# Spreading the tail frequencies late: VectorE for six token tiles, Pool for ten, and a new order of every engine's work

## The chip, the cores and the metric

The kernel runs on one core of a Trainium2 chip. Its five engines run their own instruction streams in order and meet only at semaphores: TensorE (PE in the profile, PEld its weight loads), VectorE (DVE), ScalarE (ACT), GpSimd (POOL) and SyncE (SP), which here only issues transfers. The metric is the device time in microseconds.

## What is computed

The reference, cut to what matters:

```python
def _A_ref(x, w_r, w_i):                       # spectral filter
    X = rfft2(x.astype(float32))               # over 2048 tokens and 576 features
    return irfft2(X * (w_r + 1j * w_i), s=(2048, 576)).astype(bfloat16)

def _B_ref(x, w_gate, w_up, w_down):           # 576 -> 4608 -> 576
    return (gelu(x @ w_gate) * (x @ w_up)) @ w_down

h  = x + _A_ref(layernorm(x), w_r, w_i)
h2 = h + _B_ref(layernorm(h), w_gate, w_up, w_down)
```

## The kernel before

The 2048 tokens form 16 tiles of 128 (token 16p + c lies on partition p of tile c). All Fourier transforms are matmuls with tables.

**Stage one** (to about 21 us) loads x, takes the layer norm's statistics, scales the token transform's table by 1/sigma for each tile (ATS) and multiplies (M, line 574). The tiles come in six groups (2, 2, 3, 3, 3, 3). For each group there are five products k, evicted from PSUM to U. A negated copy XN and a copy XR of x serve as operands.

**Stage two** (to about 46 us) works by 16 frequency groups: the feature transform (D its first part, d its second, line 649, evicted as CUS), a small transform (B, line 662, evicted as YS, named b), the product with the filter (T, line 674, giving TP; written "x" it reads PSUM directly and b is left out), and the transform back among the tokens of a group (V, line 682, evicted to V). The features of a filter row are 288; 256 go through V, and the last 32, the tails, go another way: Z copies them from TP to ZR, four groups together, R (line 697) multiplies them, and the result has to be spread into VR, where the inverse feature transform finds it in the layout [tile, k, group, e]. Of the 128 partitions, 32 belong to each of the four groups of a set; the spread (line 701) multiplies the product by a mask MK (1 on a group's 32 partitions, else 0), so that the other groups' places hold zeros. It is one DVE instruction for each half, over all 16 tiles: 512 elements for four groups.

**Stage three** (to about 57 us) does the inverse transform for the first six tiles (NPRE = 6): I (line 780), its copy GS, N (line 823), the addition to x (line 840), the squares for the second layer norm (s on ACT, S on DVE), q and c (square root and reciprocal), n and e (normalisation into HN, by DVE and POOL), the turn by PE (D and z, line 885, copied to HT), and the first gate and up matmuls (g and h, line 921).

**The feed-forward** (from about 57 us) is 4 blocks of 512 tokens by 36 slices of the hidden width: gate and up (line 921), gelu on ACT (929), product on DVE (930), then down (1022). The other ten tiles' inverse transform is deferred: it is put between the down matmuls of block 0 (`def_i`, line 939, reads V and VR; the first at 126 us).

**What sets the order.** Three strings of words are the order of all engines' instructions: SEQ1 for stage one, SEQF for stage two, SEQ for stage three. A word is a letter for the step, a number for its tile or group, and for some steps a letter for the engine (A ACT, D DVE, P POOL). Instructions are issued in that order on each engine, and waits follow from the data (class Prog). In SEQ1, S and Q are sums and sums of squares of a tile on ACT, B and b the statistics of a tile's halves on DVE, v q c variance, root and reciprocal of a group, m a helper of v, x the scaling, n and t the copies XN and XR, k idle matmuls that keep PE going, E an eviction to U (number 5i + j for group i and its j-th product), and F the later half of an eviction that was split. PSUM has 8 banks: `a_bank` hands them out in stage one, and in stage two `take` gives each D, B, V and R a pair of banks, by the oldest use.

The program order in every queue follows the strings, and transfers too: POOL's queue issues half of the second weight slot behind its last Z copy, then w_down's nine loads.

Of the kernel before, what the change touches and what calls it, by code (L numbers as in the profile page):

```python
# [23 lines left out]
SEQ1 = """b0 B1 Q3 t1 n0 t0 b1 k14 S3 B0 B2 v0 q0 b2 m3D c0 v1 B5 S4 b5 q1 k104 x0A M0 Q4 n1 n2 b6 c1 E2A B6 m4P B7 v2 k202 x1P q2 E1A E3A b7 B9 c2 E0A b9 M1 t2 E4A E5A b8 x2P B8 E6A b10 S13 M2 n3 E7A n4 v3 E8A B11 B10 B12 q3 Q13 c3 b11 x3A b12 t3 v4 b14 E9A B15 q4 E10A E11A m13P c4 E13A M3 t4 B14 x4P E12D E15A b15 t5 v5 E14A q5 E17A n5 E16D c5 x5A E18D E19A M4 E20D E21D M5 E24D E23A E26D F23A E22A F24A E28A E29A E25D F25A F29A E27D F26D F28D F22A F27A""".split()  # L24
# [3 lines left out]
SEQF = """D0 D1 d0 D2 d1 D3 d2 d3D B0 D4 b0D b1 D5 T1 d4 T0 d5 B1 b2 b3D T3 D6 V0 d6 B2 T2 Z0 b5 D7 D8 b4D Z1D Z2P d7 d8 Z3P T4 R0 V1 V2D B3 b6 T5 Z4D V3 b7 D10 D9 d10 Z5D T6 R1 d9 D11 V6 d11 Z6P B4 T7 b8 b9D V5 V4 B5 D12 T8 T9 D14 Z7D b10 b11 d12 T10 D13 Z8P d14 T11 d13 R2 D15 Z9P d15 B6 b12D Z10P b13 V7 T12 V9 V8 T13 B7 b14 b15x V10 Z11 Z12P T15x T14 Z13P Z14P Z15P V11 V12 V13 R3 V14 V15 R4""".split()  # L28
SEQ = """I0 I1 N0 I2 N1 s0 I3 S1 q0 N2 c0 s2 n0 N3 q1 n1 I5 e0 e1 c1 I4 z0 s3 n2 D1 e2 N5 q2 c2 N4 n3 D2 g10 e3 g00 h10 z3 h00 g20 g11 h20 g01 h11 g21 h01 h21""".split()
# [311 lines left out]
def _build(nc, A_x, A_w_r, A_w_i, B_w_gate, B_w_up, B_w_down, out):  # L341
# [194 lines left out]
    def ln1_scale(i, eng):  # L536
        c0, c1 = GROUPS[i]
        if eng == POOL:
            P.op(POOL, lambda g, c0=c0, c1=c1: g.tensor_tensor(ATS[:, c0:c1, :], ATB[:, :].unsqueeze(1).to_broadcast([128, c1 - c0, 128]),  # L539
                                                               RS1[:, c0:c1].unsqueeze(2).to_broadcast([128, c1 - c0, 128]), op=ALU.mult),  # L540
                 r=[("RS1", i), "ATB"], w=[("ATS", c) for c in range(c0, c1)])
        elif eng == ACT:
            for c in range(c0, c1):
                P.op(ACT, lambda a, c=c: a.activation(ATS[:, c, :], ATB[:, :], ACTF.Copy, scale=RS1[:, c:c + 1]),  # L544
                     r=[("RS1", i), "ATB"], w=[("ATS", c)])
        else:
            for c in range(c0, c1):
                P.op(DVE, lambda v, c=c: v.tensor_scalar(ATS[:, c, :], ATB[:, :], RS1[:, c:c + 1], None, op0=ALU.mult),
                     r=[("RS1", i), "ATB"], w=[("ATS", c)])
# [38 lines left out]
    def x_neg(i):  # L588
        c0, c1 = GROUPS[i]
        P.op(POOL, lambda g: g.tensor_scalar(XN[:, c0:c1, :], XO[:, c0:c1, 288:544], -1.0, 1.0, op0=ALU.mult, op1=ALU.mult),  # L590
             r=[("X", c) for c in range(c0, c1)], w=[("XN", c) for c in range(c0, c1)])

    def x_tail(i):
        c0, c1 = GROUPS[i]
        x = XO[:, c0:c1, 544:576]
        src = bass.AP(x.tensor, x.offset, [list(x.ap[0]), list(x.ap[1]), [0, 2], [-288, 2], [1, 32]])
        P.op(POOL, lambda g: g.tensor_copy(XR[:, c0:c1, :, :, :], src), r=[("X", c) for c in range(c0, c1)], w=[("XT", c) for c in range(c0, c1)])
# [93 lines left out]
    def st_R(q, b):  # L691
        j0, j1 = (4 * q - 3, min(4 * q + 1, NG)) if q else (0, 1)
        n, sp_, zb = j1 - j0, int(q == 0), (q - 1) % 2 if q else 2
        for k in range(4):
            for h in range(2):
                h0, vt = 64 * h, (0, 1, 1, 2)[k]
                P.op(PE, lambda t, k=k, h=h, h0=h0, vt=vt: t.matmul(bank(b + h, 0, 128, 0, 128), ZR[h0:h0 + 64, zb, k, :, :].rearrange("p a k -> p (a k)"),
                                                                    VT[h0:h0 + 64, sp_, vt, :].rearrange("p (k n e) -> p n k e", k=2, n=16), start=(k == 0), stop=(k == 3)),
                     r=[("ZR", zb, j) for j in range(4)] + ["VT"], w=[("PS", b + h)])
        for h in range(2):  # L700
            P.op(DVE, lambda v, h=h: v.tensor_tensor(VR[:, :, :, j0:j1, 4 * h:4 * h + 4].rearrange("p n k g e -> p (n k) g e"),
                                                     bank(b + h, 0, 128, 0, 128).rearrange("p (a e) -> p a e", e=4).unsqueeze(2).to_broadcast([128, 32, n, 4]),
                                                     MK[:, 0:n].unsqueeze(1).unsqueeze(3).to_broadcast([128, 32, n, 4]), op=ALU.mult),
                 r=[("PS", b + h), "MK"], w=[("V", g, 2) for g in range(j0, j1)])

# [6 lines left out]
    for w in SEQF:  # L712
# [15 lines left out]
        elif w[0] == "R":  # L728
            st_R(i, FB["R", i])
# [29 lines left out]
    vkeys = vk[0] + vk[1] + vk[2]   # L759
# [333 lines left out]
```

## Time and profile before

| | us |
|---|---|
| median of 3 runs | 488.54 |
| lowest and highest | 488.03, 488.96 |
| the profiled execution, its time | 489.37 |
| its span, first to last instruction | 487.6 |

The granted TensorE clock was 1.000. The profile names an instruction by line and engine, with the tile that it writes and those that it reads; times are counted from the start of the span. "Idle before" is the time in which the engine stood still ahead of an instruction, with what released it. Matmuls overlap, so their durations add up to more than the time that passes. The busy time of a group counts overlapping parts once; the mean of one does not.

### The profile page before, as it was taken

What the parts mean: (1) busy time and instruction counts of PE and PEld (TensorE: products, weight loads), DVE (VectorE), ACT (ScalarE), POOL (GpSimd) and SP (SyncE); (2) the same over time, 40 slices, a digit from 0 to 9 for tenths busy, and PEclk for the clock granted to TensorE, in tenths of its full rate; (3) what the DMA queues carried; (4) which work ended last, traced back from release to release, by engine and by line L of the source; (5) the groups of instructions that cost most, each with busy time, mean ns of one, the idle gap of its engine ahead of it and who ended that gap; (6) DMA issues with size and microseconds to landing.
All of it is one profiled execution on the core that took longest, in us unless ns stands there. A gap on an engine that the chain in (4) does not pass through costs nothing.

```text
span 487.6 us, 10636 instructions
## 1 busy us (share of the span) xinstructions
PE 480.4 (99%) x4726; PEld 282.1 (58%) x4726; DVE 191.9 (39%) x376; ACT 148.4 (30%) x296; POOL 33.8 (7%) x65
## 2 busy tenths in 40 slices
PE   7999999999999999999999999999999999999998
PEld 3767744444688744444577644444677444444775
DVE  6798733433576534333311144333211233333011
ACT  6988743223222222232200022332100123323000
POOL 5505420000000010000000000000000000000000
DMA  8978999100001071100000001000000000000000
GB/s 271 212 194 246 327 349 336 27 12 2 1 22 39 18 231 23 23 1 1 0 20 20 14 21 23 13 1 1 7 20 18 7 1 1 1 1 2 13 18 20
DMA packets 26174, 31.20 MB, mean 64 GB/s; under 512 B 11760, under 2 KB 17904, under 8 KB 26128
## 3 DMA queue, kind: packets, MB, share of 16 engines
q1 hardware_dynamic: 23872, 21.23, 15.5%
q0 software_dynamic: 2256, 9.29, 5.6%
q8 instruction: 37, 0.61, 0.5%
q14 instruction: 9, 0.07, 0.1%
HBM read 26.18 MB, written 2.36 MB: 59 GB/s over the span
## 4 chain that ended last, share of the span: by engine, by line
PE 93%; ACT 3%; DVE 1%; DMA 1%; SPq 0%; issue 0%; DVEq 0%
PE PS L921 57%; PE PS L1022 29%; PE PS L649 2%; DMA XO<-in_A_x_dram 1%; PE PS L939 1%; PE PS L574 1%; PE PS L662 1%; PE PS L682 1%; ACT V L639 1%; ACT U L585 1%; PE PS L957 1%; PE PS L780 0%; DVE XO L840 0%; SPq L251 0%; ACT OS L814 0%
## 5 line engine op out<-in xcount | busy, mean ns | idle before, releaser
L921 PE MATMUL PS<-HT,WG 64*128 64x512 bf16 (+1 forms) x2160 | 228.7, 371 | 0.0
L921 PEld LDWEIGHTS PS<-HT,WG 64*128 64x128 bf16 x2160 | 105.1, 94 | 121.8 <-issue 0.7
L930 DVE TENSOR_TENSOR AT<-GL,PS 128x512 bf16<-128x512 bf16 (+1 forms) x147 | 99.5, 677 | 177.5 <-ACT GL L929 177.4
L929 ACT ACTIVATE GL<-PS 128x512 bf16<-128x512 f32 (+1 forms) x147 | 86.5, 589 | 262.5 <-PE PS L921 251.3
L1022 PE MATMUL PS<-WD,AT 128*128 128x288 bf16 (+2 forms) x1152 | 144.9, 286 | 0.0
L1022 PEld LDWEIGHTS PS<-WD,AT 128*128 128x128 bf16 x1152 | 110.7, 98 | 30.6 <-ACT GL L929 1.3
L921 PE MATMUL PS<-HT,WGX 64*128 64x512 bf16 x486 | 53.4, 376 | 0.0
L1025 DVE TENSOR_TENSOR OS<-PS,XO 128x288 bf16<-128x288 f32 (+2 forms) x32 | 14.6, 457 | 94.4 <-PE PS L1022 94.3
L921 PEld LDWEIGHTS PS<-HT,WGX 64*128 64x128 bf16 x486 | 23.8, 94 | 28.7
L944 ACT ACTIVATE EB<-PS 128x288 f32<-128x288 f32 x10 | 4.1, 411 | 27.7 <-PE PS L939 27.7
L649 PE MATMUL PS<-FT,U 64*128 64x288 bf16 x160 | 12.1, 284 | 0.1
L513 DVE BATCH_NORM_STATS2 ST<-XO 128x6 f32<-128x288 bf16 x26 | 10.2, 442 | 3.4 <-DMA XO<-in_A_x_dram 3.4
L574 PE MATMUL PS<-ATS,XO 128*128 128x128 bf16 x96 | 9.2, 220 | 2.2 <-POOL ATS L539 1.2
L674 DVE TENSOR_TENSOR TP<-YS,WS 128x1152 bf16<-128x1152 bf16 x15 | 11.0, 762 | 0.1
L962 DVE TENSOR_TENSOR XO<-PS,XO 128x576 bf16<-128x576 f32 x10 | 7.6, 756 | 8.0 <-PE PS L957 8.0
L950 DVE TENSOR_TENSOR QB<-PS,EB 128x288 f32<-128x288 f32 x20 | 8.2, 452 | 3.4 <-ACT EB L944 3.3
L574 PEld LDWEIGHTS PS<-ATS,XO 128*128 128x128 bf16 x96 | 6.7, 97 | 4.8 <-ACT ATS L544 2.4
L639 ACT ACTIVATE CUS<-PS 128x576 bf16<-128x576 f32 x15 | 9.2, 652 | 0.8 <-PE PS L649 0.6
L867 DVE TENSOR_SCALAR HN<-XO,NM,RS 128x576 bf16<-128x576 bf16 (+1 forms) x28 | 9.3, 369 | 0.0
L649 PEld LDWEIGHTS PS<-FT,U 64*128 64x128 bf16 x160 | 6.6, 94 | 3.8 <-ACT CUS L639 0.7
L585 ACT ACTIVATE U<-PS 128x256 bf16<-128x256 f32 (+2 forms) x27 | 8.8, 423 | 0.1
L682 PE MATMUL PS<-VT,TP 64*128 64x128 bf16 x256 | 8.6, 217 | 0.1
(87 smaller groups left out, 205.5 us busy)
## 6 DMA issues: line engine op xcount, KB each, us to landing
WD<-in_B_w_down_dram POOLq DMA_DIRECT2D x9, 576.0 KB, 14.2
WG<-in_B_w_up_dram SPq DMA_DIRECT2D x3, 1152.0 KB, 9.1
XO<-in_A_x_dram SPq DMA_DIRECT2D x8, 288.0 KB, 5.8
WG<-in_B_w_gate_dram POOLq DMA_DIRECT2D x2, 1152.0 KB, 13.8
out_dram<-OS SPq DMA_DIRECT2D x30, 72.0 KB, 1.6
WG<-in_B_w_gate_dram SPq DMA_DIRECT2D x4, 288.0 KB, 2.9
WG<-in_B_w_up_dram SPq DMA_DIRECT2D x4, 288.0 KB, 3.3
WG<-in_B_w_gate_dram SPq DMA_DIRECT2D x1, 1152.0 KB, 6.2
```

Of the source, the lines that this page charges most:

```text
L513: P.op(DVE, lambda v: v.bn_stats(ST1[:, c, h, :], XO[:, c, 288 * h:288 * h + 288]), r=[("X", c)], w=[("ST1", c, h)])
L574: P.op(PE, lambda t, b=b, lhs=lhs, s=s, e=e, o=o, c=c: t.matmul(bank(b, 0, 128, o, o + 128), lhs, ATS[:, c, :], start=s, stop=e), r=[("X", ...
L585: fn = (lambda v: v.tensor_copy(dst, src)) if eng == DVE else (lambda a: a.activation(dst, src, ACTF.Copy))
L639: fn = (lambda v: v.tensor_copy(dst, src)) if eng != ACT else (lambda a: a.activation(dst, src, ACTF.Copy))
L649: d_done[i, o] = P.op(PE, lambda t, b=b, us=us, h0=h0, o=o, s=(not second and j == 0), e=(second and j == 1): t.matmul(bank(b, 0, 128, 0, ...
L674: P.op(DVE, lambda v: v.tensor_tensor(TP[:, i % NP, :, :, :], y4, w4, op=ALU.mult), r=rk + wkeys[sum(i >= w[1] for w in WP)], w=[("T", i % ...
L682: P.op(PE, lambda t, c=c, h0=h0, h=h, k=k, vt=vt: t.matmul(bank(b + h, 0, 128, 128 * c, 128 * c + 128), TP[h0:h0 + 64, i % NP, k // 2, k % ...
L921: op = P.op(PE, lambda t, h0=h0, kt=kt, wt=wt, b=b, s=(not second and j == 0), e=(second and j == n - 1): t.matmul(bank(b, 0, 128, c0, c1) ...
L929: P.op(ACT, lambda a: a.activation(GL[:, s2, c0:c1], bank(b0, 0, 128, c0, c1), ACTF.Gelu_apprx_tanh), r=[("PS", b0)], w=[("GL", s2)])
L930: P.op(DVE, lambda v: v.tensor_tensor(AT[:, f, c0:c1], GL[:, s2, c0:c1], bank(b0 + 1, 0, 128, c0, c1), op=ALU.mult), r=[("GL", s2), ("PS", ...
L1022: P.op(PE, lambda t, b=b, d0=d0, d1=d1, f=f, p=p: t.matmul(bank(b, 0, 128, 0, d1 - d0), AT[:, f, 128 * p:128 * p + 128], WD[:, f, d0:d1], ...
L1025: P.op(DVE, lambda v, b=b, d0=d0, d1=d1, p=p, c=c: v.tensor_tensor(OS[:, p % 2, d0:d1], bank(b, 0, 128, 0, d1 - d0), XO[:, c, d0:d1], op=A ...
```

## The change

The tails of the first six tiles are spread as before, by DVE, but over 6 tiles: 192 elements for a half of four groups. For the other ten tiles (or for group 0, which needs no spread, all 16) the product is copied as it is, 160 elements for both halves, into the place of the set's first group (`ev` with the engine that the word names; ACT where it names none). Four instructions on POOL (`spread`), emitted behind the issues of w_down, then multiply it by each column of MK into its place, the first group's own place last. A new key, VD, orders that against the deferred tiles' matmuls.

The words for R get an engine; n and t too; a DVE scaling becomes one instruction for a group instead of one for each tile. The three order strings are new: among other things x0 goes from ACT to DVE, x1 from POOL to ACT, n5 from POOL to DVE; of the 16 CUS copies 4 instead of 1 are DVE's; of the YS copies 3 instead of 5 are DVE's, 11 instead of 10 ACT's, and 2 instead of 1 left out by a direct product; of the Z copies 4, 3 and 9 instead of 2, 4 and 10 are ACT's, DVE's and POOL's; evictions to U move by a few.

The code:

```diff
     def ln1_scale(i, eng):
         c0, c1 = GROUPS[i]
-        if eng == POOL:
-            P.op(POOL, lambda g, c0=c0, c1=c1: g.tensor_tensor(ATS[:, c0:c1, :], ATB[:, :].unsqueeze(1).to_broadcast([128, c1 - c0, 128]),
+        if eng != ACT:
+            P.op(eng, lambda g, c0=c0, c1=c1: g.tensor_tensor(ATS[:, c0:c1, :], ATB[:, :].unsqueeze(1).to_broadcast([128, c1 - c0, 128]),
...
-    def x_neg(i):
+    def x_neg(i, eng):
...
-    def x_tail(i):
+    def x_tail(i, eng):
...
-    def st_R(q, b):
+    def st_R(q, b, eng):
         j0, j1 = (4 * q - 3, min(4 * q + 1, NG)) if q else (0, 1)
...
-        for h in range(2):
-            P.op(DVE, lambda v, h=h: v.tensor_tensor(VR[:, :, :, j0:j1, 4 * h:4 * h + 4].rearrange("p n k g e -> p (n k) g e"),
-                                                     bank(b + h, 0, 128, 0, 128).rearrange("p (a e) -> p a e", e=4).unsqueeze(2).to_broadcast([128, 32, n, 4]),
-                                                     MK[:, 0:n].unsqueeze(1).unsqueeze(3).to_broadcast([128, 32, n, 4]), op=ALU.mult),
+        c0 = NPRE if q else 0
+        for h in range(2 if q else 0):
+            P.op(DVE, lambda v, h=h: v.tensor_tensor(VR[:, 0:c0, :, j0:j1, 4 * h:4 * h + 4].rearrange("p n k g e -> p (n k) g e"),
+                                                     bank(b + h, 0, 128, 0, 8 * c0).rearrange("p (a e) -> p a e", e=4).unsqueeze(2).to_broadcast([128, 2 * c0, n, 4]),
+                                                     MK[:, 0:n].unsqueeze(1).unsqueeze(3).to_broadcast([128, 2 * c0, n, 4]), op=ALU.mult),
                  r=[("PS", b + h), "MK"], w=[("V", g, 2) for g in range(j0, j1)])
+        ev(eng, VR[:, c0:NT, :, j0, :].rearrange("p n k (h e) -> p h (n k) e", h=2), banks(b, 2, 128)[:, :, 8 * c0:].rearrange("p h (a e) -> p h a e", e=4),
+           [], [("PS", b), ("PS", b + 1), ("VD", j0)] + ([] if q else [("V", 0, 2)]))
+
+    def spread(j):
+        gs = list(range(1 + j, NG, 4))
+        src, dst = (VR[:, NPRE:NT, :, g:NG:4, :].rearrange("p n k g e -> p (n k) g e")[:, :, 0:len(gs), :] for g in (1, 1 + j))
+        P.op(POOL, lambda g: g.tensor_scalar(dst, src, MK[:, j:j + 1], None, op0=ALU.mult), r=[("VD", g) for g in range(1, NG, 4)] + ["MK"], w=[("VD", g) for g in gs])
...
     vk = [[("V", g, c) for g in range(NG)] for c in range(3)]
+    vk += [[("VD", g) for g in range(NG)]]
...
-                         r=vk[ch] + ["DP"], w=[("PS", b + o)])
+                         r=vk[ch if ch < 2 else 3] + ["DP"], w=[("PS", b + o)])
...
         P.dma(POOL, WD[:, 4 * j:4 * j + 4, :], wdv[:, 4 * j:4 * j + 4, :], f"wd{j}", w=[("WD", j)])
+    for j in (1, 2, 3, 0):
+        spread(j)
```

The orders, cut to their pieces around the steps of which the prediction speaks (the words are those of the strings, the lines are broken here):

```diff
 SEQ1
-b0 B1 Q3 t1 n0 t0 b1 k14 S3 B0 B2 v0 q0 b2 m3D c0 v1 B5 S4 b5 q1 k104 x0A M0 Q4 n1 n2 b6 c1 E2A
-B6 m4P B7 v2 k202 x1P q2 E1A E3A b7 B9 c2 E0A b9 M1 t2 E4A E5A b8 x2P B8 E6A b10 S13 M2
...
-E17A n5 E16D c5 x5A E18D E19A M4 E20D E21D M5 E24D E23A E26D F23A E22A F24A E28A E29A E25D F25A
-F29A E27D F26D F28D F22A F27A
+b1 S3 t1P k14 B1 b0 B0 Q3 B2 v0 m3D n0P b2 q0 S4 c0 v1 k104 t0P x0D q1 B5 Q4 b5 c1 M0 B6 b6 E2A
+n1P E1A n2P m4P b7 x1A t2P v2 E0A B9 q2 B7 M1 c2 b11 b10 E4A b9 E5A x2P E8A E3A b8 E6A S13
...
+E15D q5 n5D E18A c5 x5A E17D M4 E19D E21D E24D E23A E20A M5 E22A F23A F24D E25A E26A E27D F26D
+E28A E29A F25A F27D F22D F29D F28A
 SEQF
-D0 D1 d0 D2 d1 D3 d2 d3D B0 D4 b0D b1 D5 T1 d4 T0 d5 B1 b2 b3D T3 D6 V0 d6 B2 T2 Z0 b5 D7 D8
...
-B7 b14 b15x V10 Z11 Z12P T15x T14 Z13P Z14P Z15P V11 V12 V13 R3 V14 V15 R4
+D1 D0 D3 d0D d1 D2 d3 d2D B0 D5 b1 b0 d5 B1 T1 b3 T0 D4 Z0 b2D D6 d4 T2 Z1P D7 d6 d7D B2 T3 Z2
+b4 V2 b5 T4 D8 D9 d8 d9D T5 V0 V3 B3 b6x b7 T6x D10 V5 V1D d10 B4 D12 Z3D Z4P b8 D11 T7
...
+B6 D14 b12x D15 Z9 b13 Z10P T12x d14 Z11P R2D d15 T13 V12 V9
+B7 b15 b14D V10 Z12P Z13D V13 V8 T15 V11 V15 T14 R3D Z14P Z15P V14 R4
 SEQ
-I0 I1 N0 I2 N1 s0 I3 S1 q0 N2 c0 s2 n0 N3 q1 n1 I5 e0 e1 c1 I4 z0 s3 n2 D1 e2 N5 q2 c2 N4 n3 D2 g10
+I0 I1 N0 I2 N1 s0 I3 S1 q0 N2 c0 e0 s2 N3 q1 n1 I4 n0 e1 I5 c1 n2 D1 s3 z0 N4 e2 q2 c2 N5 n3 D2 g10
```

More of the change, by code (lines that the diff above doesn't have):

```diff
@@ L596, in x_tail @@
         src = bass.AP(x.tensor, x.offset, [list(x.ap[0]), list(x.ap[1]), [0, 2], [-288, 2], [1, 32]])
-        P.op(POOL, lambda g: g.tensor_copy(XR[:, c0:c1, :, :, :], src), r=[("X", c) for c in range(c0, c1)], w=[("XT", c) for c in range(c0, c1)])
+        P.op(eng, lambda g: g.tensor_copy(XR[:, c0:c1, :, :, :], src), r=[("X", c) for c in range(c0, c1)], w=[("XT", c) for c in range(c0, c1)])
     ENG = {"A": ACT, "D": DVE, "P": POOL}
@@ L728, in _build @@
         elif w[0] == "R":
-            st_R(i, FB["R", i])
+            st_R(i, FB["R", i], e)
     wdv = B_w_down[:, :].rearrange("(c p) d -> p c d", p=128)
```

16 lines of the change are left out of this document (6 added, 10 removed).

## Prediction

> **What bounds the kernel now.** I read the busy time by stage first, then the chain that ended last in order of time, then the timeline of each engine up to 57 us, and last the groups of instructions with their shapes kept apart. By stage (the stretch and its length, then busy us of PE, PEld, DVE, ACT and POOL, the clock, the DMA share and rate):
>
> ```profile
> 0.00:21.50 21.50, 17.80 (x180) 11.14 (x180) 16.05 (x66) 17.20 (x55) 12.69 (x30) 1.00 0.88 249
> 21.50:46.30 24.80, 24.05 (x572) 17.41 (x568) 22.47 (x36) 22.82 (x42) 5.62 (x11) 1.00 0.78 205
> 46.30:57.50 11.20, 10.76 (x108) 7.96 (x108) 8.89 (x21) 8.55 (x18) 4.55 (x10) 1.00 1.02 332
> 57.50:169.00 111.50, 111.50 (x1066) 67.84 (x1066) 54.36 (x105) 35.00 (x73) 7.73 (x12) 1.00 0.30 97
> ```
>
> From 57.5 us on PE has no gap until the down projection of the last tile, so nothing that the change does there can gain; it can only lose. What can be won or lost is the moment at which that unbroken stretch begins. Before it, a busy PE says little, since its records overlap; DVE and ACT are both over 90% busy in the second stage. The chain, in order of time (start, length, what):
>
> ```profile
> 45.12 1.09 ACT V L639 x2
> 46.35 1.66 PE PS L780 x12
> ...
> 54.81 0.76 ACT OS L814 x2
> 55.60 0.30 ACT RS L847
> 56.09 0.66 DVE XO L840
> ...
> 57.14 0.45 PE PS L885 x5
> 57.59 68.58 PE PS L921 x674
> ```
>
> The first token tiles' inverse transform (L780) starts when ScalarE's last copy of V is out. So the kernel's time is, to a shift, the end of ScalarE's list of copies in the second stage, plus a tail of 11.2 us. The two joints of that list, and what DVE does beside it:
>
> ```profile
> 17.58 3.25 DVE L585 CAST U<-PS 128x384 bf16<-128x384 f32 x9
> 18.59 2.89 ACT L585 ACTIVATE U<-PS 128x384 bf16<-128x384 f32 x11
> 21.72 1.90 ACT L639 ACTIVATE CUS<-PS 128x576 bf16<-128x576 f32 x3 [0.25 <-PE PS L649]
> 23.22 0.76 DVE L639 CAST CUS<-PS 128x576 bf16<-128x576 f32 x1 [2.38 <-PE PS L649]
> 24.65 1.43 DVE L674 TENSOR_TENSOR TP<-YS,WS 128x1152 bf16<-128x1152 bf16 x2
> ...
> 43.53 2.68 ACT L639 ACTIVATE V<-PS 128x512 bf16<-128x512 f32 x5
> 44.38 2.54 DVE L701 TENSOR_TENSOR VR<-PS,MK 128x512 bf16<-128x512 f32 x4
> 46.35 0.77 PE L780 MATMUL PS<-DT,V 128*128 128x288 bf16 x5 [0.59 <-ACT V L639]
> ```
>
> ACT leaves stage one at 21.48 (18.59 + 2.89), starts the second list 0.24 later and ends it with five copies of V back to back at 46.21. DVE idles 2.38 us at the opening and ends with the spread tails at 46.92. PE then waits 0.59 for V; the sixth matmul, the first on VR, comes five matmuls later, when VR is just done.
>
> **The change, part by part.** Prices of the second stage: the groups of ACT and DVE in it (mean ns stands after the busy us), then the spread by shape, and two rows for new copies.
>
> ```profile
> L639 ACT ACTIVATE CUS<-PS 128x576 bf16<-128x576 f32 x15 | 9.2, 652 | 0.8 <-PE PS L649 0.6
> L639 ACT ACTIVATE V<-PS 128x512 bf16<-128x512 f32 x15 | 8.3, 603 | 0.3 <-PE PS L682 0.2
> L639 ACT ACTIVATE YS<-PS 128x576 bf16<-128x576 f32 x10 | 6.5, 654 | 0.7 <-PE PS L662 0.6
> L639 ACT ACTIVATE ZR<-TP 128x128 bf16<-128x128 bf16 x2 | 0.6, 312 | 0.0
> ...
> L674 DVE TENSOR_TENSOR TP<-YS,WS 128x1152 bf16<-128x1152 bf16 x15 | 11.0, 762 | 0.1
> L639 DVE CAST YS<-PS 128x576 bf16<-128x576 f32 x5 | 3.8, 754 | 0.1
> L674 DVE TENSOR_TENSOR TP<-PS,WS 128x1152 bf16<-128x1152 f32 x1 | 1.4, 1358 | 0.0
> L639 DVE CAST CUS<-PS 128x576 bf16<-128x576 f32 x1 | 0.8, 758 | 2.4 <-PE PS L649 2.4
> ```
> ```profile
> L701 DVE TENSOR_TENSOR VR<-PS,MK 128x512 bf16<-128x512 f32 x6 | 4.1, 689 | 0.3 <-PE PS L697 0.2
> L701 DVE TENSOR_TENSOR VR<-PS,MK 128x384 bf16<-128x384 f32 x2 | 1.1, 557 | 0.0
> L701 DVE TENSOR_TENSOR VR<-PS,MK 128x128 bf16<-128x128 f32 x2 | 0.6, 288 | 0.0
> L585 ACT ACTIVATE U<-PS 128x256 bf16<-128x256 f32 x10 | 3.3, 404 | 0.0
> L930 DVE TENSOR_TENSOR AT<-GL,PS 128x256 bf16<-128x256 bf16 x6 | 2.5, 421 | 3.2 <-ACT GL L929 3.1
> L867 DVE TENSOR_SCALAR HN<-XO,NM,RS 128x576 bf16<-128x576 bf16 x16 | 6.8, 424 | 0.0
> ```
>
> *The spread itself.* Before: six spreads of 512 elements, two of 384, two of 128: 6 x 0.689 + 2 x 0.557 + 2 x 0.288 = 5.82 us of DVE. After: six of 192 elements and two of 144 (six token tiles), by the line through the 128 and 384 rows 0.355 and 0.305, so 2.74; and the unspread copies, 160 elements each, which no row shows: between 0.288 and 0.557, taken as 0.32, near the smaller shape. Three of them are DVE's (0.96), one ACT's, and group 0 becomes one 256-element copy on ACT (0.404). DVE is relieved of 5.82 - 2.74 - 0.96 = 2.1 us.
>
> *The new shares of the second stage.* DVE: 14 products instead of 15 (-0.76), a second one straight from PSUM (+1.36), two YS copies fewer (-1.51), three CUS copies more (+2.27), one ZR copy fewer (under 0.3): with the spread -2.1, its list is about 0.9 shorter. ACT: the sum of its means was 15 x 0.652 + 15 x 0.603 + 10 x 0.654 + 2 x 0.312 = 25.99 us, run in 22.82 busy us, since copies overlap (0.878). With 12, 15, 11 and 4 copies and the 0.404 it is 25.72, times 0.878 22.58: **-0.25**. Bounds: 0 (the saved CUS copies stood where ACT waited anyway) and -0.6 (the whole 0.27 at full price, and the two ZR copies hidden in waits). So the relief of DVE reaches ACT's list hardly at all, and ACT's list is what ends last.
>
> The row of five V copies gives (2.68 - 0.603)/4 = 0.52 us for one behind another. [...]
>
> *Stage one.* Its rows:
>
> ```profile
> 1.46 5.79 PE L559 MATMUL PS<-ZD 128*128 128x512 bf16 x18 [1.46 <-POOL ZD L444]
> ...
> 8.67 0.15 DVE L534 RECIPROCAL RS<-RS 128x2 f32<-128x2 f32 x1
> 10.03 0.30 ACT L529 ACTIVATE RS<-MV,EPT 128x3 f32<-128x3 f32 x1 [1.18 <-DVE MV L525]
> 10.51 0.10 PEld L574 LDWEIGHTS PS<-ATS,XO 128*128 128x128 bf16 x1 [1.50 <-POOL ATS L539]
> ```
>
> c1 (8.67) now stands ahead of the statistics that wait for tile 6, and x1 goes from POOL to ACT, so M1 need not wait for POOL until 10.51. x0 becomes one DVE product (0.42 by the 256-element row); M0 gains little, as 18 idle matmuls hold PE until 7.25. What counts is ACT: in the 1.18 us that it idled before 10.03 it now does x1 and the copies E1 and E0. Behind 10.33 its list has two 256-element copies fewer, one of 384 more and one of 192 fewer: -0.81 for two copies, at most +0.4 for 192 elements: **-0.4**, the last U copy at 21.1. Bounds: 0 (q2 still comes at 10.03, and M3's scaling stands behind more copies) and -0.8. DVE takes n5 (768 elements; the 576-element row gives 0.424, so 0.5) and one short U copy more for a longer one fewer: its U copies end about 20.83 + 0.3 = 21.1 too. POOL's share, two steps lighter, ends nothing.
>
> *The opening of the second stage.* Before: D0 D1 d0, so the first CUS copy came 0.24 behind the last U copy. After: D1 D0 D3 and only then d0, d1. D3's PSUM pair holds E27 and E28, and F28 is ACT's last U copy; PE, in order, therefore does D3 (six matmuls in three pairs, some 0.4), d0 and d1 (0.25 each) behind it, with 0.25 until the result can be read: ACT's first copy starts 1.2 us behind the last U copy instead of 0.24, and another 0.2 goes before b1. Before, ACT lost 0.9 in three gaps here (0.25, then 0.25 and 0.40 up to 24.92); after, 1.4: **+0.5**. DVE copies d0 and d2 in what was its 2.38 us gap, which is why it is not the full 1.0. Bounds: 0 and +1.0.
>
> *The rest of the second stage.* T6 and T12 read PSUM directly, 1.36 us each on DVE and behind both halves of B3 and B6; V5 and b15 on ACT then wait some 0.35 each, against 0.37 and 0.17 before: **+0.1** (-0.3 to +0.6). The tail: T14's ZR copies, R4 and two spreads of 0.305 end near the sixth matmul of L780, as before: 0 (-0.1 to +0.4).
>
> *Tail to 57.5 us.* PE is busy 10.76 of 11.20, so 0.4 is the most to win. z0's copies now stand behind s3 on ACT, which delays the first gate matmuls by about 0.3; but the next point, z3 at 57.14, hangs on s3, q2 (55.60), the addition and the normalisation, and ACT does the same instructions ahead of q2 in either order: 0 (-0.2 to +0.3).
>
> *The feed-forward.* Four spreads on POOL, 640 elements each at most, stand behind the issues of w_down.
>
> ```profile
> 56.52 6.81 POOL L251 DMA_DIRECT2D WD<-in_B_w_down_dram x9
> 36.47 2.39 POOL L639 COPY ZR<-TP 128x128 bf16<-128x128 bf16 x3 [3.56 <-DVE TP L674]
> 44.38 0.65 POOL L639 COPY ZR<-TP 128x128 bf16<-128x128 bf16 x2 [1.52 <-DVE TP L674]
> ```
>
> They start at 63.3; their reader is the first deferred tile at 126.17 (57.59 + 68.58). Even at several us they have nearly 60 to hide in: 0. Uncovered they would cost their own length. The w_gate loads on POOL's queue stay behind its last ZR copy, and the w_up loads on SP's behind the last product that reads W, now T14; both come no later than that list ends: 0.
>
> **Sum:** -0.4 + 0.5 - 0.25 + 0.1 + 0 = -0.05, call it -0.1. The profiled execution took 489.37 (span 487.6 and 1.77 around it), so it would take 489.3; it lies 0.83 above the median of 488.54, and against that median the forecast is **488.4 us**.
>
> **The rivals.** *A, DVE was the bound.* DVE has 0.4 us of waits between 23.22 and 46.92, less than ACT, and VR's last product ends just where VR is first read. If ACT only waited on DVE, the 0.9 of shorter list and the 0.3 of earlier start come through: -1.2, 487.3. Against it: the matmul that waited 0.59 waited for ACT's V. Chance 0.25.
> *B, slower: the opening.* If the U copies end no earlier than 21.48 (term one at 0), D3 behind F28 costs its whole 0.96, with the DVE copies no help since B0 needs d1 from ACT, and the two direct products add 0.6: +0.96 + 0.6 - 0.25 = +1.3, 489.8. It decides once ACT's last U copy ends after about 21.4. Chance 0.22.
> *C, POOL and DVE exclude each other.* POOL's ZR copies took 0.80 each beside DVE's products from SBUF (36.47) and 0.33 beside products from PSUM (44.38). If n5, now on DVE, meets POOL's ATS or XR work in stage one, it and DVE's U copies behind it slip by up to 0.5: 488.9. Chance 0.08. [...]
> *D, the change does nothing of what it says:* only the orders matter, if the spread was never late; that is the forecast itself, whose terms are nearly all orders.
>
> **How the numbers follow.** Forecast 0.45, C 0.08, A 0.25, B 0.22. Within 0.2% (0.98 us, about what a measurement of this kernel can tell from no change) lie the forecast and C, less a little at their edges: same 0.51. Faster 0.26, slower 0.23. Eight in ten: from a little below A to B, 487.0 to 489.9; the forecast alone has 487.6 to 489.3.
>
> **What would show it.** ACT's last U copy at 21.1 and its first CUS copy 1.2 behind it: terms one and two. The inverse transform (L780) starting at 46.2 to 46.4 behind a V copy of ACT: the bound is ACT. If it starts near 45.3, A; after 47, B. DVE's busy time in the second stage about 1 lower with more waiting. The stretch of L921 without a gap from some 11.2 us after the start of L780. What would make all of it wrong is a wait that I have not priced in the 24 us of interleaved copies: any one of a hundred reordered steps late by half a microsecond moves the sum by as much as its largest term.

## The result: 0.7 us slower, and the profile after

| us | before | after |
|---|---|---|
| median (19 runs each) | 488.43 | 489.15 |
| lowest and highest | 487.89, 489.10 | 488.91, 489.82 |
| the profiled execution, its time | 489.37 | 489.15 |
| its span | 487.6 | 487.4 |

The ratio is 1.0016, 95% interval 1.0009 to 1.0023: slower by 0.72 us, 0.4 to 1.1. The forecast was 488.4 us, no change. The two profiles shown say the opposite of the medians: the execution of before that was profiled is 0.94 above its own median, and the one of after is at its median. So the profiles can't be subtracted as they stand; part of the work was to find which of before's 489.37 us were its own. A second profile of before, at its median (**before_again**, 488.41, span 486.6), serves from here on.

The busy time by stage of after (columns as before: stretch, length, PE, PEld, DVE, ACT, POOL, clock, DMA share and rate):

```profile
0.00:21.50 21.50, 17.83 (x195) 11.90 (x197) 17.12 (x69) 17.05 (x56) 11.26 (x28) 1.00 0.91 248
21.50:46.30 24.80, 23.70 (x562) 17.08 (x557) 22.12 (x38) 22.86 (x44) 4.67 (x11) 1.00 0.76 204
46.30:57.50 11.20, 10.51 (x110) 7.99 (x109) 8.38 (x20) 8.63 (x19) 4.86 (x10) 1.00 1.02 340
```

In the second row DVE is busy 0.35 less and ACT as much as before, but this can't be read as the relief: the window is fixed while the work shifts (in before_again, a microsecond earlier, the same window has 23.11 and 21.99). Between fixed events, from the first matmul of the feature transform to the first inverse matmul, DVE is busy 23.20 in before_again and 23.44 in after, ACT 24.12 and 23.52. The groups of the new and moved steps, with their shapes (busy us, mean ns):

```profile
L635 ACT ACTIVATE V<-PS 128x512 bf16<-128x512 f32 x15 | 8.1, 606 | 0.7 <-PE PS L678 0.7
...
L635 ACT ACTIVATE CUS<-PS 128x576 bf16<-128x576 f32 x12 | 7.5, 653 | 1.8 <-PE PS L645 1.7
...
L708 POOL TENSOR_SCALAR VR<-VR,MK 128x640 bf16<-128x640 bf16 x3 | 5.7, 1889 | 0.2
...
L698 DVE TENSOR_TENSOR VR<-PS,MK 128x192 bf16<-128x192 f32 x6 | 2.1, 356 | 0.4 <-PE PS L693 0.3
...
L635 DVE CAST VR<-PS 128x160 bf16<-128x160 f32 x3 | 1.0, 324 | 0.1
...
L698 DVE TENSOR_TENSOR VR<-PS,MK 128x144 bf16<-128x144 f32 x2 | 0.6, 307 | 0.2 <-PE PS L693 0.2
```

The prices of the spread were right to 0.01 us (0.355, 0.305 and 0.32 forecast). POOL's four spreads took 7.15 us together, and hide. ACT waited 1.8 for CUS instead of 0.8, and 0.7 for V instead of 0.3. Where, on ACT's timeline at both joints, and on PE's:

```profile
17.69 2.48 ACT L581 ACTIVATE U<-PS 128x192 bf16<-128x192 f32 x10
21.46 1.26 ACT L635 ACTIVATE CUS<-PS 128x576 bf16<-128x576 f32 x2 [1.29 <-PE PS L645]
...
45.09 0.60 ACT L635 ACTIVATE V<-PS 128x512 bf16<-128x512 f32 x1 [0.46 <-PE PS L678]
```
```profile
43.88 0.23 PE L678 MATMUL PS<-VT,TP 64*128 64x128 bf16 x2
44.49 0.57 PE L678 MATMUL PS<-VT,TP 64*128 64x128 bf16 x14 [0.37 <-issue]
...
45.83 0.77 PE L785 MATMUL PS<-DT,V 128*128 128x288 bf16 x5 [0.55 <-ACT V L635]
...
55.27 1.70 PE L926 MATMUL PS<-HT,WG 64*128 64x256 bf16 x28 [0.33 <-ACT RS L852]
56.91 0.45 PE L890 MATMUL PS<-IDT,HN 128*128 128x128 bf16 x5
```

ACT's last V copy no longer runs back to back with the one before it: it waits for V14's matmuls, and among these PE stood still for 0.37 us without a releaser that the profile could name ("issue"). Such a stop is called a stand below. The first gate matmul waits 0.33. The chain ends as before, with the same piece from its start on:

```profile
57.36 68.58 PE PS L926 x674
```

From that point on before and after are equal to 0.01 us in their profiles: 427.72 us to the last addition of the output in both (57.59 to 485.31, 57.36 to 485.08). So the feed-forward neither gained nor lost, and all that follows is about the first 57 us, in three pieces: to ACT's last U copy, from there to the first inverse matmul (I), and from there to the unbroken stretch.

### The profile page after: what moved, and what is told of

Same layout as the page of the kernel before. It is cut to its first block, busy times and chain, and to the rows that moved or that the text cites. A ratio compares the mean times of both kernels' runs of the same rounds, so it can differ in the third digit from the quotient of the medians.

```text
span 487.4 us, 10641 instructions
## 1 busy us (share of the span) xinstructions
PE 479.6 (98%) x4726; PEld 281.8 (58%) x4726; DVE 192.1 (39%) x379; ACT 148.1 (30%) x298; POOL 38.2 (8%) x66
## 4 chain that ended last, share of the span: by engine, by line
PE 95%; ACT 2%; DVE 2%; DMA 1%; issue 0%
PE PS L926 58%; PE PS L1029 29%; PE PS L645 2%; PE PS L678 2%; PE PS L570 1%; PE PS L944 1%; PE PS L658 1%; ACT U L581 1%; DMA XO<-in_A_x_dram 1%; PE PS L962 1%; PE PS L785 0%; DVE ST L513 0%; ACT OS L819 0%; DVE XO L845 0%; ACT GS L635 0%
## 5 line engine op out<-in xcount | busy, mean ns | idle before, releaser
L819 ACT ACTIVATE JD<-XO,NM 128x576 bf16<-128x576 bf16 x10 | 7.7, 767 | 3.1 <-DVE XO L967 3.1
```

## The experiments

Two theories stood at the start. **The orders** cost what they cost by themselves: the opening of the second stage, and z0 behind s3 in the third. **The spread**: its new copies, or the work that it moves, upset ACT or PE. All times are against before in the same set of runs (31 to 35 runs of it, medians 488.54 to 488.67); the intervals of single kernels are some 0.4 us wide to each side, so the small parts are read from the traces, and the times are their check.

**Before_again**, nothing edited: is before's profile a fair one?

> The kernel before, unchanged, for a second profile of it. Theory (late landing): the profiled execution of before was 0.94 us above its own median because x for tile 6 landed late (DVE waited until 8.29, ACT 1.18 us for the variance until 10.03); another execution at the median has these waits under 0.4 us, ACT's last U copy near 20.5 instead of 21.48 and the unbroken gate/up stretch from about 56.7 instead of 57.59. Rival (landing is as shown, the change loses behind 57 us): the same waits again, last U copy near 21.5, the stretch from 57.5. Both: time within 0.2 us of 488.43.

Measured 0.9997 (0.9988 to 1.0005). Its ACT timeline at the two joints:

```profile
8.57 0.39 ACT L585 ACTIVATE U<-PS 128x256 bf16<-128x256 f32 x1
9.01 0.30 ACT L529 ACTIVATE RS<-MV,EPT 128x3 f32<-128x3 f32 x1
...
17.55 2.89 ACT L585 ACTIVATE U<-PS 128x384 bf16<-128x384 f32 x11
20.67 1.91 ACT L639 ACTIVATE CUS<-PS 128x576 bf16<-128x576 f32 x3 [0.23 <-PE PS L649]
```

The 1.18 us in which ACT waited for DVE's variance ahead of 10.03 in the first profile aren't there: the root comes at 9.01, and the last U copy ends at 20.44 instead of 21.48. From there to I (45.39) are 24.95 us, to the stretch (56.64) another 11.25, as in the first profile (24.87, 11.24). The whole excess of that profile was in stage one, as the first of the two expectations had it.

**Spread_only**: the new code of the spread under the three old orders.

```diff
-... T4 R0 V1 ... T6 R1 d9 ... d13 R2 D15 ... V13 R3 V14 V15 R4
+... T4 R0 V1 ... T6 R1D d9 ... d13 R2D D15 ... V13 R3D V14 V15 R4
```

> The new spread (six tiles on DVE, ten copied and spread by POOL in the feed-forward, same engines for R as in the change) under the three old orders. Theory (the loss is in the orders, DVE's relief reaches the end of the second stage little): 0 to 0.4 us faster than before. Rival (the spread itself costs, by ACT's two more copies and POOL's 7.4 us in the feed-forward): 0.5 to 0.9 us slower, like the change.

(R0 and R4 name no engine, so ACT copies them; the four spreads on POOL are those of the change.) 1.0005 (0.9996 to 1.0013): neither the gain of up to 0.4 us that was expected nor the rival's loss of 0.5 or more, though the interval reaches into both. I comes 25.37 behind the last U copy, but 0.36 of it is a stand of PE, at 29.91; without it 25.01.

**Spread_dve**: the same with R0 and R4 on DVE too.

> The new spread under the old orders, with all of R's copies on DVE (R0 and R4 too). Theory (ACT's list ends last; the two copies on ACT are what the spread cost in spread_only, where the stretch from the last U copy to L785 was 25.37 instead of 24.9): the stretch is 24.8 to 24.95 again, the time within 0.2 of before. Rival (DVE is the bound, as my rival A had it, and its 2 us of relief show once ACT carries no copy): the stretch falls to 24.4 or less, the time 0.4 or more below before.

1.0001 (0.9992 to 1.0010), 24.84 and 11.21. The spread itself, by the traces of the two, costs 0 to 0.1 (by their times 0.05 and 0.24, not to be told from 0); and taking some 2 us of work from DVE gains nothing either. The theory of the spread falls, and so does rival A: DVE was not the bound.

**Seq_only**: before with the new third order.

```diff
-SEQ = """I0 I1 N0 I2 N1 s0 I3 S1 q0 N2 c0 s2 n0 N3 q1 n1 I5 e0 e1 c1 I4 z0 s3 n2 D1 e2 N5 q2 ...
+SEQ = """I0 I1 N0 I2 N1 s0 I3 S1 q0 N2 c0 e0 s2 N3 q1 n1 I4 n0 e1 I5 c1 n2 D1 s3 z0 N4 e2 q2 ...
```

> The kernel before with the new order of stage three alone. Theory (stage three loses 0.28): that stretch 11.53 us instead of 11.25, the time 0.2 to 0.4 above before. My forecast: 0 to 0.1 above before.

1.0007 (0.9998 to 1.0015): +0.33 in the medians. The trace has 24.88 and then 11.64 instead of 11.25. PE's timeline at that place, of seq_only and then of before_again:

```profile
54.58 0.44 PE L885 MATMUL PS<-IDT,HN 128*128 128x128 bf16 x5
55.44 1.71 PE L921 MATMUL PS<-HT,WG 64*128 64x256 bf16 x28 [0.42 <-ACT RS L847]
57.07 0.45 PE L885 MATMUL PS<-IDT,HN 128*128 128x128 bf16 x5
```
```profile
54.04 0.44 PE L885 MATMUL PS<-IDT,HN 128*128 128x128 bf16 x5
54.41 1.70 PE L921 MATMUL PS<-HT,WG 64*128 64x256 bf16 x28
56.18 0.45 PE L885 MATMUL PS<-IDT,HN 128*128 128x128 bf16 x5
```

The first gate matmuls read z0's copy. In before_again that copy is out before the turn of the next tile is done, and PE goes on; with z0 behind s3 PE waits, and from there to z3 (56.18, 57.07) it has no gap any more, so the wait goes through whole. (The row names ACT's root; the copy stands right ahead of it on ACT, and the weights that these matmuls also wait for had landed by 44.4 in the profiles of before and after.)

**After_old3**: after with the old third order (the same edit the other way round).

```diff
-SEQ = """I0 I1 N0 I2 N1 s0 I3 S1 q0 N2 c0 e0 s2 N3 q1 n1 I4 n0 e1 I5 c1 n2 D1 s3 z0 N4 e2 q2 ...
+SEQ = """I0 I1 N0 I2 N1 s0 I3 S1 q0 N2 c0 s2 n0 N3 q1 n1 I5 e0 e1 c1 I4 z0 s3 n2 D1 e2 N5 q2 ...
```

> The changed kernel with the old order of stage three (z0 ahead of s3, n0 ahead of the addition of tile 3). Theory (stage three loses 0.28: in the changed kernel PE waits 0.33 for z0's copy behind s3, and the stretch from the first L785 to the unbroken stretch is 11.53 us instead of 11.25): that stretch is 11.25 again, the time about 0.3 below the changed kernel, 0.4 to 0.5 above before. My forecast (ACT does the same ahead of q2 in either order: 0): no difference, 0.7 above before.

1.0011 (1.0000 to 1.0022); behind I 11.21 instead of 11.53. The 0.3 of the third stage is its new order, shown from both sides; that it is z0 behind s3 in it is read from the rows, as no run moves these two words alone.

**Seq1_only** and **seq1_again**: before with the new first order, and x, n and t taking the engine that the word names.

```diff
-b0 B1 Q3 t1 n0 t0 b1 k14 S3 B0 B2 v0 q0 ... k104 x0A M0 ... F28D F22A F27A
+b1 S3 t1P k14 B1 b0 B0 Q3 B2 v0 m3D n0P ... x0D q1 ... M0 ... F27D F22D F29D F28A
```

> Only the new order of stage one, the spread and the other two orders as before. Theory (late landing): stage one's gain that I forecast, 0.4, was the late x of one execution; at most 0.3 faster, last U copy of ACT between 20.1 and 20.5. My forecast of stage one: 0.4 us or more faster. Rival (the new stage one is what loses, by n5 and x0 on DVE): 0.5 or more slower.

> Seq1_only once more. Its time (1.0014) was more than its trace accounts for (opening 0.4, stage one about 0.1: 1.0010 at most). Theory (the rest was chance): 1.0005 to 1.0010. Rival (the new first order costs more than the one trace shows, for instance by a late M0 in most executions): 1.0013 or more, and M0 at 8 us or later with the last U copy past 21.

1.0014 (1.0005 to 1.0023) and 1.0010 (0.9995 to 1.0025): not the gain of up to 0.3 us that was expected, but a loss of the rival's size. Both traces have a first CUS copy 0.67 to 0.69 behind ACT's last U copy instead of 0.23, although the second order is the old one, and I 25.30 and 25.29 behind it instead of 24.9. That looks like a cost of 0.35 to 0.4 at the end of the evictions, but it is the boundary that moved. PE's rows, of before_again and then of seq1_again, with the first feature transform D and the first small transform:

```profile
19.14 2.99 PE L649 MATMUL PS<-FT,U 64*128 64x288 bf16 x40
22.07 0.68 PE L662 MATMUL PS<-CUS,BT 64*64 64x288 bf16 x16
```
```profile
19.35 3.04 PE L645 MATMUL PS<-FT,U 64*128 64x288 bf16 x40
22.33 0.69 PE L658 MATMUL PS<-CUS,BT 64*64 64x288 bf16 x16
```

PE works through the transforms without a gap in the rows, and the first small transform comes 2.93 and 2.98 behind the first D. What changed is where ACT's last U copy lies: 1.30 behind the first D in before_again (20.44), 0.93 in seq1_again (20.28). ACT is done 0.37 earlier and waits that much longer for PE. From the first D to I there are 26.25 us in before_again and 26.22 in both profiles of seq1, so behind the first D the new first order costs nothing. The first piece differs between the two by the start of the first product M0:

```profile
1.46 6.90 PE L555 MATMUL PS<-ZD 128*128 128x512 bf16 x18 [1.46 <-POOL ZD L444]
8.20 0.22 PE L570 MATMUL PS<-ATS,XO 128*128 128x128 bf16 x1
```
```profile
1.46 5.76 PE L555 MATMUL PS<-ZD 128*128 128x512 bf16 x18 [1.46 <-POOL ZD L444]
7.20 0.23 PE L570 MATMUL PS<-ATS,XO 128*128 128x128 bf16 x1
```

The 18 idle matmuls ahead of M0 take 6.90 us in the one and 5.76 in the other, and the last U copy ends at 21.26 and 20.29: the same 13.06 and 13.09 behind M0. The rival (the new order costs more than its trace, by a late M0 as a rule) isn't settled: seq1_again's profile has an early M0, but it is the fastest of that kernel's 11 executions (488.59, median 489.43), and the loss of 0.5 to 0.7 us in the times is one that these traces don't show behind the first D.

**After_k9**: after with five idle matmuls fewer (k14 to k9), to let M0 start earlier.

```diff
-b1 S3 t1P k14 B1 b0 B0 Q3 B2 v0 m3D n0P
+b1 S3 t1P k9 B1 b0 B0 Q3 B2 v0 m3D n0P
```

> The changed kernel with 13 instead of 18 idle matmuls ahead of M0. Its first scaling is out at about 7.0, so the idle matmuls hold it in each execution that warms after 4.5 us. Theory: 0.2 to 0.5 below the changed kernel (488.6 to 489.0). Rival (warming later): no gain.

1.0015 (1.0006 to 1.0024), M0 at 7.29, last U copy 20.64: no gain, against the 0.2 to 0.5 that were expected. Its 13 idle matmuls took 5.73 us, as long as the 18 of seq1_again.

**After_old1** and **after_old13**: after with the old first order, and with the old first and third.

```diff
 after_old1: SEQ1
-b1 S3 t1P k14 B1 b0 B0 Q3 B2 v0 m3D n0P ... F27D F22D F29D F28A
+b0 B1 Q3 t1P n0P t0P b1 k14 S3 B0 B2 v0 q0 ... F28D F22A F27A
 after_old13: SEQ1 as in after_old1, SEQ as in after_old3
```

> The changed kernel with the old order of stage one. Theory (the new stage one with its joint to stage two costs about 0.7): 488.4 to 488.6, at most 0.2 above before, ACT's gap between last U and first CUS copy about 0.7 or less. Rival (the loss of the opening is SEQF's, D3 ahead of d0 and d1, whatever stage one is): the gap stays over 1.1 us, the time 0.5 to 0.8 above before.

> The changed kernel with the old orders of stages one and three: the new spread and the new order of stage two alone. Theory (stage one 0.7, stage three 0.28, second stage with its spread a gain of 0.2 to 0.3): 488.0 to 488.4, 0.1 to 0.4 faster than before. Rival (the loss sits in the second stage): 0.4 or more slower than before.

1.0012 (1.0003 to 1.0021) and 1.0004 (0.9996 to 1.0013): after_old1 has its rival's time and its gap on ACT (1.13), and after_old13 gains nothing, against the 0.1 to 0.4 that were expected. The second piece is 25.22 and 25.21 in the two, the third 11.53 and 11.21. So the new second order costs some 0.3 with the old first order: from the first D to I 26.51 and 26.50. With the new first order it costs nothing there: after and after_old3 have 26.22 and 26.24 without PE's stand, like seq1 with the old second order. That is why the two new orders together make no more of the second piece than either alone.

**Open_fix**: after with d0 and d1 ahead of D3 again.

```diff
-D1 D0 D3 d0D d1 D2 d3 d2D B0
+D1 D0 d1 d0D D3 D2 d3 d2D B0
```

> The changed kernel with one edit: the opening of stage two is D1 D0 d1 d0D D3 D2 instead of D1 D0 D3 d0D d1 D2, so that the first two second halves do not stand behind D3, whose banks hold ACT's last U copy. Theory (opening): the gap on ACT between its last U copy and its first CUS copy falls from 1.29 to under 0.7 us, and the time falls by 0.3 to 0.7 us from the changed kernel's 489.15, to 488.4 to 488.8. Rival (the loss lies in the interleaved copies behind it): the gap shrinks, the time stays at 489.0 to 489.3.

1.0016 (1.0007 to 1.0024): no gain, where 0.3 to 0.7 were expected. ACT's first CUS copy came 0.67 behind the last U copy instead of 1.29, but the second then waited 0.57, and I stands 25.33 behind. The words d0 and d1 were not what the opening lost by; mending the one gap opened the next, and from the first D to I it has 26.26.

**Best1** and **best2**: after_old13 with another opening, and that with k9 for k14.

```diff
-D1 D0 D3 d0D d1 D2 d3 d2D B0
+D0 D1 d0D D2 d1 D3 d2D d3 B0
```

> The new spread and the new order of stage two under the old orders of stages one and three, with the opening of stage two mended (D0 D1 d0D D2 d1 D3 d2D d3: one second half behind two first ones). Theory (the opening is what the second stage loses; behind it the new shares and the relieved DVE gain): the gap on ACT falls to 0.3 us, the stretch from the last U copy to L785 to 24.3 to 24.6 us instead of 24.9, the time 0.2 to 0.6 below before. Rival (ACT's list is as long as before, the relief of DVE buys nothing): the stretch stays at 24.8 to 25.2, the time within 0.2 of before.

> As best1, with 9 instead of 14 idle matmuls at the start (13 instead of 18 ahead of M0). Theory (idle matmuls hold M0: they run 0.427 apart until PE warms, at 4.4 to 7.4 us in the profiles so far, and end as late as 8.2 while the first scaling is out by 7.5): M0 at 7.3 to 7.6 in every execution, 0.1 to 0.4 below best1, less spread among the runs. Rival (with fewer idle matmuls PE warms later or cools before M0): M0's matmuls or the idle ones stay at the slow spacing behind 7.5 us, no gain or up to 0.5 slower.

0.9998 (0.9989 to 1.0007) and 0.9995 (0.9986 to 1.0004). Best1 has 24.80 and 11.20: with the old first order, D0 and D1 first and DVE copying d0, the loss of the second stage is gone (from the first D 26.09). But the gain of 0.2 to 0.6 that was expected of best1 didn't come: neither beats before by more than the measurement can tell. Best2's profile (489.74) has a stand of 1.01 in V14.

**New1_best**: best1 with the new first order.

```diff
-b0 B1 Q3 t1P n0P t0P b1 k14 S3 B0 B2 v0 q0 ... F28D F22A F27A
+b1 S3 t1P k14 B1 b0 B0 Q3 B2 v0 m3D n0P ... F27D F22D F29D F28A
```

> The changed kernel with the old order of the third stage and the opening of best1 (D0 D1 d0D D2 d1 D3 d2D d3), the first order new. Theory (opening and third stage are the loss): lastU to I matmuls near 24.9 to 25.2, then 11.21; time 1.0000 to 1.0006, some 0.5 us under the changed kernel. Rival (the new first order is the loss): 1.0010 or more, since best1 with the old first order took 0.9998.

1.0011 (1.0002 to 1.0020). First CUS copy 1.30 behind again, I 25.49 behind, of which 0.23 is a stand; from the first D 26.19 without it. The theory (1.0000 to 1.0006) missed, and the time is the rival's (1.0010 or more): the new first order loses, though behind the first D its trace has only 0.10 more than best1's.

**After_again** and **after_again2**: after, nothing edited. Of the profiles ahead of these two, five have a stand, and in after and after_old3 it is at one instruction.

> The changed kernel once more, nothing edited. Theory (PE's instruction block late): in the changed kernel's profile and in after_old3's PE stands 0.36 to 0.37 us at the same place, ahead of the third matmul of V14, and in best2 at the same count of PE instructions (726 or 727 matmuls); each time it goes on 1.32 to 1.38 us behind the end of one packet of the instruction queue. So here it stands again at that place if the packet that starts near 42 us ends later than some 1.35 before 44.4, and then goes on 1.35 behind it; I matmuls minus last U copy 25.25 plus what PE stood there; behind it 11.53; time 1.0013 to 1.0018. Rival (a hiccup of single executions): a wait for nothing at some other place, or with no packet ahead of it.

> The same kernel a third time, for a third profile at the same place: the same expectation. If both profiles show the wait, it is a part (0.3 to 0.4) of the 0.72; if neither does, the 0.72 has to come from the orders alone: 0.35 in the second stage, 0.28 in the third, 0 to 0.2 in the first.

1.0021 (1.0012 to 1.0031) and 1.0017 (1.0008 to 1.0026). PE's timeline in after_again, then its DMA queues in the tenth of a microsecond from 43.1 (packets, MB, share of 16 engines):

```profile
44.37 0.23 PE L678 MATMUL PS<-VT,TP 64*128 64x128 bf16 x2
45.66 0.57 PE L678 MATMUL PS<-VT,TP 64*128 64x128 bf16 x14 [1.05 <-issue]
```
```profile
q8 instruction: 1, 0.02, 67.5%
```

And in after_again2, there from 41.6:

```profile
44.25 0.84 PE L678 MATMUL PS<-VT,TP 64*128 64x128 bf16 x16
```
```profile
q8 instruction: 1, 0.02, 60.0%
```

The queue q8 that the page calls "instruction" moves single packets of 16,384 bytes (37 packets and 0.61 MB in the whole run). The share gives its length (67.5% of 16 engines over 0.1 us is 1.08 us), so in after_again it was in by 44.23, in after_again2 by 42.61. Put together for every profile with such a stand:

| us | packet starts | it is in | PE goes on | behind it | PE stood | matmuls recorded before |
|---|---|---|---|---|---|---|
| after | 42.15 | 43.11 | 44.49 | 1.38 | 0.37 | 726 |
| after_old3 | 42.45 | 43.42 | 44.74 | 1.32 | 0.36 | 726 |
| after_again | 43.15 | 44.23 | 45.66 | 1.43 | 1.05 | 726 |
| new1_best | 41.75 | 43.19 | 44.47 | 1.28 | 0.23 | 726 |
| best2 | 43.05 | 44.26 | 45.60 | 1.34 | 1.01 | 727 |
| spread_only | 27.25 | 28.56 | 29.91 | 1.35 | 0.36 | 347 |

PE goes on 1.28 to 1.43 us behind the end of the packet (the starts are known to 0.05), at one count of recorded matmuls, wherever the words put it: in best2, with five idle matmuls fewer, six matmuls later in V14. Where the packet was in earlier (after_again2, after_k9), PE runs through; the nearest without a stand is after_old13, where PE comes to that place 1.23 behind the packet. That PE waits there for its own next instructions, and that the packet brings them, is my reading: the rows show only that the two come together, and no run took the packet away. Between the counts of 347 and 726 lie 379 matmuls and as many weight loads, and spread_only's trace has three packets that start between 31.5 and 42.7: some 126 matmuls with their loads to a packet. Over the whole run of before the 37 packets start 126.6 recorded matmuls apart on average, so they follow PE's progress. The rival of a hiccup falls. At this place 5 of 11 profiles with the new second order have a stand and none of 7 with the old one. The new order makes it likelier, but the rows don't show that it needs it: some 126 matmuls earlier, at about 600 recorded ones, the packet starts 0.7 to 2.7 us behind PE (in before_again 1.09: it starts at 40.95, is in by 41.93, and PE comes to the count of 726 only at 44.0). PE takes 4.1 us for these 126 matmuls with the old order and 3.9 with the new in most profiles (80 V matmuls in a row, 41.33 to 43.76 in after, instead of 64), so the room is some 0.2 smaller. What varies more is the packet: in the three profiles of the same kernel it starts 2.11, 2.66 and 1.24 behind that count, and PE stands 0.37, 1.05 and 0. What sets this delay isn't shown by the trace.

All profiles in one table; "last U" is ACT's last U copy, "stood" the stand, and the last column but one takes it off:

| | ratio | M0 | last U | last U to I | stood | without | I to stretch |
|---|---|---|---|---|---|---|---|
| before, before_again | 0.9997 | 7.51, 7.62 | 21.48, 20.44 | 24.87, 24.95 | 0 | 24.9 | 11.24, 11.25 |
| spread_dve | 1.0001 | 7.72 | 20.80 | 24.84 | 0 | 24.84 | 11.21 |
| spread_only | 1.0005 | 7.97 | 21.08 | 25.37 | 0.36 | 25.01 | 11.21 |
| seq_only | 1.0007 | 8.33 | 21.00 | 24.88 | 0 | 24.88 | 11.64 |
| seq1_only, seq1_again | 1.0014, 1.0010 | 8.20, 7.20 | 21.26, 20.29 | 25.30, 25.29 | 0 | 25.3 | 11.25, 11.24 |
| best1 | 0.9998 | 8.50 | 21.17 | 24.80 | 0 | 24.80 | 11.20 |
| best2 | 0.9995 | 7.61 | 20.88 | 25.86 | 1.01 | 24.85 | 11.21 |
| after_old13 | 1.0004 | 8.31 | 20.95 | 25.21 | 0 | 25.21 | 11.21 |
| after_old1 | 1.0012 | 7.64 | 20.35 | 25.22 | 0 | 25.22 | 11.53 |
| new1_best | 1.0011 | 7.20 | 20.28 | 25.49 | 0.23 | 25.26 | 11.21 |
| after_old3 | 1.0011 | 7.34 | 20.42 | 25.67 | 0.36 | 25.31 | 11.21 |
| open_fix | 1.0016 | 7.25 | 20.75 | 25.33 | 0 | 25.33 | 11.53 |
| after_k9 | 1.0015 | 7.29 | 20.64 | 25.25 | 0 | 25.25 | 11.53 |
| after | 1.0016 | 7.09 | 20.17 | 25.66 | 0.37 | 25.29 | 11.53 |
| after_again, after_again2 | 1.0021, 1.0017 | 7.16, 7.46 | 20.65, 20.53 | 26.35, 25.34 | 1.05, 0 | 25.3 | 11.53, 11.53 |

## Why the prediction was wrong, step by step

The last link was read rightly: in every profile of the changed kernel the first inverse matmul follows ACT's V copy, and the feed-forward adds nothing. But the bound was not the length of ACT's list. From the first feature matmul (D) to the first inverse matmul (I) there are 26.2 to 26.3 us, without PE's stand, in before_again (ACT busy 24.12, DVE 23.20), in spread_only (24.34 and 21.66) and in after (23.52 and 23.44): neither 1.5 us less on DVE nor 0.6 less on ACT shortens the piece. What does bound it no run here shows. Of the terms of the sum:

- **Stage one, forecast -0.4: did not come.** This is the first step that failed, in two ways. The term filled 1.18 us in which ACT waited, and that wait was one execution's; the profile of before had said that it lay 0.83 over its median, and I carried that over as a shift of the end and not as a doubt about its waits. And it took the end of ACT's U copies for the end of the stage. Against PE's first D that end did come 0.36 earlier (0.91 to 0.93 behind it in all nine profiles with the new first order, 1.29 to 1.30 in all nine with the old), but nothing followed: the first CUS copy waits for PE, and the first D itself came no earlier (19.24 to 20.34, mean 19.63, against 19.06 to 20.19, mean 19.61). M0 is at 7.09 to 8.20 instead of 7.51 to 8.50, held in after by x0, which took 0.63 on DVE and not the 0.42 of the forecast (6.41 to 7.04); the first D comes 12.14 to 12.57 behind M0 instead of 11.34 to 11.98 (12.68 in before's first profile). No run isolates what takes this time.

  The times say that the new first order loses: the four sets of kernels that differ in it alone (after and after_old1, after_old3 and after_old13, new1_best and best1, seq1 and before) lie 0.3 to 0.6 us apart, and less what the traces show behind the first D, 0.5 to 0.6 are left for stage one. Each interval is 0.4 wide or more to each side, and the profiles show none of it in their means, so its size stays open, from 0 to 0.6 us.
- **Second stage, forecast +0.5 - 0.25 + 0.1 = +0.35: the size came, by luck.** From ACT's last U copy to I the piece grew from 24.9 to 25.2 to 25.35 without PE's stand, and the first CUS copy came 1.29 behind that copy (forecast 1.2). But 0.36 of it is the other side of the term before: ACT was done earlier and waited longer. From the first D to I nothing grew: 26.17 and 26.25 in before, 26.17 to 26.27 in the profiles with both new orders. The gap that I had blamed on D3 costs its 0.25 only with the old first order (26.50 and 26.51); with the new one open_fix closes it and gains nothing. So the forecast's two largest terms were one shift of ACT's copies, counted twice with opposite signs. The -0.25 for ACT's shorter list was sized rightly (from D to I ACT is busy 23.52 in after and 23.74 in seq1_again, which has the old second order: -0.22), but I comes no earlier for it. Rival B's price of 1.3 didn't come: the first piece did not end late, and of the 1.8 and 0.7 that ACT waited for CUS and V in after, 1.29 and 0.46 lie at the two joints and not behind the direct products.
- **Not in the sum: PE's stand.** In 5 of the 11 profiles with the new second order PE stood, 0.23 to 1.05 us; over the 11 a mean of 3.02 / 11 = 0.27 (over the three of the changed kernel itself 0.47). It goes through to I, as the last V copies wait for V14. My text said that an unpriced wait in the interleaved part would be what upsets it; this is one that no order string shows.
- **Third stage, forecast 0: +0.28.** The second step that failed. I saw that z0's delay would hold the first gate matmuls by 0.3, and set it to nothing because z3 at 57.14 hangs on s3 and q2. In after the normalised tile for z3 is ready at 56.39 (55.97 + 0.42 on DVE), and z3 starts at 56.91, when PE is through with the gate matmuls that began late. The limit that should have hidden the delay was past 0.52 before PE came, so nothing hid it.
- **Feed-forward, 0: right,** though each of POOL's spreads took 1.5 to 1.9 us.
- **Rivals A and C:** A falls with spread_dve. C: in after n5 ran on DVE from 16.07 for 0.54 us (0.5 forecast), with no wait ahead of it. That POOL and DVE exclude each other no run shows: the rows of before have the two lengths of the ZR copies (0.80 us at 36.47, 0.33 at 44.38) and not their cause.

Sum by these: 0 to 0.6 (stage one) + 0 (second stage) + 0.27 + 0.28 = 0.55 to 1.15, against +0.72, +0.83 and +1.0 in the three measurements of the same kernel. What stays open is how much of it the new first order loses ahead of the first D and by which word, and what sets the delay of a packet of q8.

## What to carry to other kernels

Before a wait in a trace is counted as something to win, see whether that execution is a usual one: compare its time with the median, and take a second profile if it is off. When a delay is called hidden by the next limit, work out from the rows when that next limit is ready, not which steps it depends on. A piece that is measured from one engine's last copy grows when that copy comes early: measure it from what the next engine does, too. Relief of an engine counts only as far as the next event comes earlier for it; that the last link of a chain is an engine's copy doesn't make that engine's list the bound.

## What the runs showed of the hardware

- **PE stood still until 1.28 to 1.43 us behind the end of a packet of the queue that the page calls "instruction".** These packets have 16,384 bytes and come one at a time in before and after; at the stands they were 0.96 to 1.44 us long, while weights load. The page shows a stand as "issue", 0.23 to 1.05 us, at a count of 726 or 727 recorded matmuls in five profiles and of 347 in one. In after it comes behind a dense run of short matmuls (80 in 2.43 us, from 41.33). That PE had run out of instructions there is a reading that rests on these coincidences; no run takes the packet away.
- **The speed-up of the idle matmuls comes at a different time in each execution.** They start 0.43 us apart and later 0.22, and the switch (the "warming" of the expectations) comes at 4.4 us (after) to 7.4 (after_old13), so the 18 of them took 5.47 (after_old3) to 7.01 us (after_old13), at a granted clock of 1.00 in the rows throughout. In four profiles M0 starts 0.22 behind the start of the last of them (after_again at 7.16, after_again2 at 7.46, seq1_only at 8.20, after_old13 at 8.31), so there they hold it, over a range of a microsecond; in the others it starts later behind them. No run shows what sets the moment of the switch.
- **POOL took longer over fewer elements:** its spread of 640 elements took 1.889 us, while its negated copy of 768 took 0.832. The spread's places are runs of four elements and its factor is a column of MK; the copy has longer runs and a fixed factor. No run tells which of the two it is:

```profile
L586 POOL TENSOR_SCALAR XN<-XO 128x768 bf16<-128x768 bf16 x3 | 2.5, 832 | 0.5 <-DMA XO<-in_A_x_dram 0.3 <-POOL XN L586 0.2
```
